# A masked attention and rational feed-forward kernel: the rational function in pieces of 2048 columns, small VectorE chains put into the order link by link, and new order tables

## The chip, the core and the metric

The program runs on one core of one Trainium2 chip. The metric is the device time of one execution in microseconds; the median of three runs of the kernel before is 1252.32 us (1250.29 to 1256.62). Lower is better. Five engines matter: PE (TensorE, matrix products; its weight loads are listed apart as PEld), DVE (VectorE), ACT (ScalarE), POOL (GpSimd) and SP (SyncE, which here only issues transfers).

## What is computed

Attention over 8 batches of 8 heads, 576 positions, 64 values a head, in which scores below the row's maximum less tau are dropped, and after it a feed-forward layer whose activation is a rational function:

```python
scores = scale * np.matmul(q, k.transpose(0, 1, 3, 2))
thresh = np.max(scores, axis=-1, keepdims=True) - tau
scores = np.where(scores >= thresh, scores, -1000000000.0)
attn = softmax(scores)                       # written out in the reference
x = (attn @ v).transpose(0, 2, 1, 3).reshape(4608, 512)
h = x @ w_in                                 # 512 -> 2048
P = a[0] + a[1] * h + a[2] * h * h + a[3] * h ** 3
Q = 1.0 + abs(b[0]) * abs(h) + abs(b[1]) * h * h
out = (P / (Q + 1e-06)) @ w_out              # 2048 -> 512
```

## The kernel before, in words

**Attention.** A unit is one pair of heads and one block of 128 queries (the last block of a pair holds the 64 remaining queries of both heads). Per unit PE makes the scores (L938, L945, L949), DVE takes the maximum (L955, L957), a small operation makes the threshold (L962 on ACT or L964 on DVE), ACT masks (L970) and exponentiates with a sum (L974), DVE inverts the sum (L985), the weights are split into a high half `hi` (L398 on ACT or L400 on DVE) and a low half (L996 on DVE), two transposing transfers on SP turn them, and PE multiplies by the two halves of V (L1069). For the first units PE itself transposes (L1019, L1024) and multiplies in f32 (L1050).

**Feed-forward.** Work goes by chunks of 256 tokens, and for each chunk by steps of eight blocks of 128 columns of w_in (`NB = 8`). There are 38 steps (the last one of a chunk at the end of the run is cut into smaller ones by `TAIL`). In a step PE makes h in split half precision (L1316), ACT scales it out of the banks (L1326), and then the rational function runs on the step's 2048 columns in *pieces*. Eleven operations make a piece: A (L1333 on ACT or L1335 on DVE), r2 (L1341), q (L1345), r3 (L1355), ln (L1348, ACT), inv (L1351, ACT), e (L1359), n (L1363), g (L1367), gh (L398 on ACT or L400 on DVE) and gl (L1381). All those without an engine named are on DVE. Then PE multiplies by w_out (L1390). `PIECE = 2` makes a piece of 1024 columns, so that a full step has two. The three buffers of a step (h, q, r) come from a pool `t` of seven.

**Scales.** Each chunk has a gain chain: squares (L1175 or L1177), a sum on PE (L1182), a maximum and two bit operations on DVE (L1185, L512, L513), seven one-element operations on POOL (L1198 to L1204), two on DVE (L1209, L1210) and two on POOL (L1244, L1245). The weights' and V's scales end in a chain of six one-element operations on DVE, the function `power` (L501 to L507).

**The order.** Nothing in the program is in the order of the code. Each operation is handed to a planner (`Plan`) with its engine or engines, an assumed duration, a key, what it comes after and which buffers it takes and drops. The planner walks through an imagined time, takes on each engine the startable operation with the smallest key, chooses between ACT and DVE where both are allowed (`FLEX`), and so writes one fixed list for each engine. Wherever its imagined PE stands idle for long enough it puts filler products of the identity matrix into PE's list (`f_warm`, L1557):

```python
n = int((t - free[e]) * WARM / 0.22)     # WARM = 0.6
```

An operation of the planner may hold several instructions; those stand together in the list. Before the change `power` and its relatives are such blocks, for instance

```python
nc.vector.tensor_reduce(cn[:, i:i + 1], bank(hb), AX.X, ALU.max)
power(cn[:, i:i + 1], place(hs)[:, 2:3], 14, sw[:, i:i + 1], ...)
sd = op("DVE", 1.735, key + K["cs"], f_cs, [sd], [hs], [hb, hs])
```

Of the kernel before, what the change touches and what calls it, by code (L numbers as in the profile page):

```python
# [88 lines left out]
K = {"f1": 3.009, "f2": 0.12, "f4": -0.954, "f6": -9.013, "load": -13.706, "junk": 0.862, "sq": 0.34, "cn": -8.632, "cs": 0.764,  # L89
     "s1": -0.486, "s2": -1.589, "wh": 6.869, "wl": -2.379, "wc": -5.563, "vl": 2.383, "vc": 7.9, "vh": 4.017, "qk": -0.767,  # L90
     "max": -2.213, "thr": -0.29, "pre": -0.907, "sum": 2.6, "rec": 2.33, "rec2": -0.863, "diag": -3.135, "tr": -4.968,
# [4 lines left out]

SHIFT_STEPS = {0: -0.394, 1: 4.873, 2: -2.335, 3: -0.077, 4: 1.467, 5: -1.25, 6: -0.993, 7: 1.754, 8: -0.124, 9: 1.878,
# [3 lines left out]

SHIFT_UNITS = {0: -1.536, 1: 0.546, 2: 0.586, 3: 0.677, 4: 1.109, 5: 0.804, 6: -5.595, 7: -0.393, 8: -6.844, 9: -1.995,
# [20 lines left out]
LAM = 0.375  # L123

START = {"ACT": 4.989, "DVE": 3.836}
START_END = 94.259
EARLY = {"ACT": 1.437, "DVE": 3.934}
EARLY_END = 3405.643
PRICE = {"ACT": 1.353, "DVE": 13.322}

TOL = {"PE": 0.066, "ACT": 0.0, "DVE": 0.045, "POOL": 0.1, "DMA": 0, "GD": 0}
# [2 lines left out]
SHARE, SET_OUT, LANDS = (1.47, 0.75), 1.22, (0.68, 1.5)
# [213 lines left out]
def masked_attention_rational_ffn(  # L348
# [119 lines left out]
    def monic():  # L468

        t, u, a3 = (co_[:, i:i + 1] for i in range(6, 9))
        nc.vector.tensor_scalar(t, b0, 2.0 ** -40, TINY, ALU.mult, ALU.max)
        nc.vector.tensor_tensor(t, b1, t, ALU.max)
        nc.vector.reciprocal(u, t)
        nc.vector.tensor_tensor(bc, b0, u, ALU.mult)
        nc.vector.tensor_scalar(qc, u, QC, None, ALU.mult)
        nc.vector.tensor_reduce(t, cf[:, 0:3], AX.X, ALU.max, apply_absolute_value=True)
        nc.vector.tensor_scalar(t, t, TINY, TINY, ALU.mult, ALU.max)  # L480
        nc.vector.tensor_scalar(osc, cf[:, 3:4], 0.0, 2.0, ALU.is_ge, ALU.mult)
        nc.vector.tensor_scalar(osc, osc, -1.0, None, ALU.add)
        nc.vector.scalar_tensor_tensor(a3, cf[:, 3:4], osc, t, ALU.mult, ALU.max)
        nc.vector.tensor_tensor(a3, a3, osc, ALU.mult)
        nc.vector.scalar_tensor_tensor(osc, a3, -1.0, u, ALU.mult, ALU.mult)
        nc.vector.reciprocal(a3, a3)
        nc.vector.tensor_scalar(co_[:, 0:3], cf[:, 0:3], a3, None, ALU.mult)

        nc.vector.tensor_scalar(co_[:, 12:14], co_[:, 3:5], TINY, None, ALU.max)
        nc.vector.reciprocal(co_[:, 12:14], co_[:, 12:14])  # L490
        nc.vector.tensor_single_scalar(co_[:, 9:12].bitcast(I32), co_[:, 0:3].bitcast(I32), 0x7FFFFFFF, ALU.bitwise_and)
# [4 lines left out]
    def power(square, p2, up, inv, s):

# [8 lines left out]
        if s is not None:  # L506
            nc.vector.reciprocal(s, inv)  # L507
# [1092 lines left out]
```

## Time and profile before

| | before |
|---|---|
| median of 3 runs, us | 1252.32 |
| the profiled execution's own time, us | 1245.89 |
| its span, first to last instruction, us | 1243.8 |
| granted TensorE clock, mean | 0.999 |
| PE busy, us (share of the span) | 1201.5 (97%) |
| DVE busy | 1188.5 (96%) |
| ACT busy | 1139.5 (92%) |
| POOL busy | 383.2 (31%) |

The profiled execution is 6.4 us below the median of the runs and 2.1 us lie outside its span. A profile row names the line, the engine, the operation, the tiles as out<-in, their shape, the count, the busy time and the mean duration of one instruction; behind it the idle time of the engine just ahead of these and what ended it. The profile's durations of neighbouring instructions on DVE and ACT overlap a little, so that what one instruction costs its engine is read from start to start in the timeline.

### The profile page before, as it was taken

The page shows a single profiled execution, that of the slowest core. Times are in us where ns is not written, and L with a number is a line of the kernel's source. Part 1 is how long each engine was busy: PE and PEld are TensorE (multiplying, and loading weights), DVE is VectorE, ACT ScalarE, POOL GpSimd, SP SyncE. Part 2 cuts the span into 40 slices and gives each one's busy share as a digit, 9 for nine tenths or more (in the row PEclk, how much of TensorE's full clock was granted, in tenths as well). Part 3 has the DMA queues.
Part 4 walks back from the last instruction along what each step waited for, and adds up shares of the span by engine and source line. Part 5 has one row for each costly group of instructions (what it writes and reads, how often), then busy time and mean ns, then how long its engine had stood idle before and what let it go on. Part 6 is the DMA issues. An engine that isn't in the chain of part 4 may idle for free. (4 is left out here: it accounts for less than half of the span.)

```text
span 1243.8 us, 25741 instructions
## 1 busy us (share of the span) xinstructions
PE 1201.5 (97%) x9537; PEld 791.3 (64%) x9542; DVE 1188.5 (96%) x1733; ACT 1139.5 (92%) x2174; POOL 383.2 (31%) x651
## 2 busy tenths in 40 slices
PE   8887899999999999999999999999999999999998
PEld 6556566566666656756666666665756575766754
DVE  6999989999999999999999999999999999999976
ACT  7999999999999999999988999999999799989733
POOL 2220313153042521524044333343416261710300
PEclk9999999999999999999999999999999999999999
DMA  7662264668467675566525575667655665524300
GB/s 231 208 224 91 84 140 81 129 144 168 83 119 139 132 153 93 121 133 131 103 65 102 119 166 112 131 127 143 144 93 123 109 139 125 108 54 84 66 18 17
DMA packets 341484, 147.75 MB, mean 119 GB/s; under 512 B 314224, under 2 KB 325424, under 8 KB 341360
## 3 DMA queue, kind: packets, MB, share of 16 engines
q1 hardware_dynamic: 320944, 92.06, 39.5%
q0 software_dynamic: 20096, 53.47, 15.1%
q8 instruction: 75, 1.23, 0.4%
q10 hardware_dynamic: 320, 0.59, 0.2%
q14 instruction: 49, 0.40, 0.1%
HBM read 54.69 MB, written 9.44 MB: 52 GB/s over the span
## 5 line engine op out<-in xcount | busy, mean ns | idle before, releaser
L1390 PE MATMUL banks<-wp,t 128*128 128x512 f16 x1728 | 394.9, 380 | 3.8 <-DVE t L1381 3.6
L1316 PEld LDWEIGHTS <-wi 128*128 128x128 f16 x3456 | 333.5, 98 | 76.0 <-issue 23.9
L1316 PE MATMUL banks<-x,wi 128*128 128x256 f16 x3072 | 360.8, 273 | 3.8 <-ACT t L1326 3.1
L1390 PEld LDWEIGHTS <-t 128*128 128x128 f16 x1728 | 163.6, 98 | 204.3 <-issue 22.2
L970 ACT ACTIVATE e<-banks,st 128x576 f32<-128x576 f32 x288 | 210.9, 740 | 14.4 <-DVE st L964 7.5
L974 ACT ACTIVATE e<-e,cf 128x576 f32<-128x576 f32 x288 | 222.7, 781 | 0.1
L996 DVE SCALAR_TENSOR_TENSOR e<-e,st,hi 128x576 f16<-128x576 f32 x252 | 201.7, 809 | 2.5 <-ACT hi L398 2.4
L955 DVE TENSOR_REDUCE st<-banks 128x2 f32<-128x1152 f32 x128 | 172.4, 1348 | 9.0 <-PE banks L949 8.1
L398 ACT ACTIVATE hi<-e,st 128x576 f16<-128x576 f32 x221 | 169.6, 773 | 7.9 <-DVE st L985 4.9
L949 PE MATMUL banks<-KK,QQ 64*128 64x512 f32 x512 | 144.6, 641 | 0.0
L1069 PEld LDWEIGHTS <-V 128*64 128x64 f16 x2520 | 103.7, 111 | 56.4 <-issue 52.9
L1069 PE MATMUL banks<-pT,V 128*64 128x256 f16 (+1 forms) x2520 | 120.8, 249 | 3.9 <-DMA pT<-e 1.2
L1326 ACT ACTIVATE t<-banks,hsc 128x512 f32<-128x512 f32 (+1 forms) x192 | 107.1, 582 | 13.3 <-PE banks L1316 11.4
L1348 ACT ACTIVATE t<-t,co 128x1024 f32<-128x1024 f32 (+1 forms) x73 | 82.9, 1137 | 20.6 <-DVE t L1345 16.3
L1341 DVE SCALAR_TENSOR_TENSOR t<-t,co 128x1024 f32<-128x1024 f32 (+1 forms) x73 | 92.0, 1260 | 4.8 <-ACT t L1326 4.8
L1359 DVE SCALAR_TENSOR_TENSOR t<-t,co,t 128x1024 f32<-128x1024 f32 (+1 forms) x73 | 92.1, 1262 | 3.5 <-ACT t L1351 3.4
L1355 DVE SCALAR_TENSOR_TENSOR t<-t,co,t 128x1024 f32<-128x1024 f32 (+1 forms) x73 | 92.1, 1261 | 0.1
L1367 DVE SCALAR_TENSOR_TENSOR t<-t,co,t 128x1024 f32<-128x1024 f32 (+1 forms) x73 | 91.9, 1260 | 0.1
L1345 DVE SCALAR_TENSOR_TENSOR t<-t,co 128x1024 f32<-128x1024 f32 (+1 forms) x73 | 91.9, 1260 | 0.0
L1381 DVE SCALAR_TENSOR_TENSOR t<-t,gsc,t 128x1024 f16<-128x1024 f32 (+1 forms) x73 | 90.8, 1260 | 0.2
L1363 DVE SCALAR_TENSOR_TENSOR t<-t,t 128x1024 f32<-128x1024 f32 (+1 forms) x73 | 87.6, 1201 | 0.3
L1333 ACT ACTIVATE t<-t 128x1024 f32<-128x1024 f32 x72 | 75.7, 1052 | 1.8 <-DVE t L1381 1.5
(184 smaller groups left out, 1614.8 us busy)
## 6 DMA issues: line engine op xcount, KB each, us to landing
KK<-in_kT_dram POOLq DMA_DIRECT2D x94, 144.0 KB, 2.9
t<-in_w_in_dram POOLq DMA_DIRECT2D x8, 1024.0 KB, 6.1
t<-in_w_out_dram POOLq DMA_DIRECT2D x8, 1024.0 KB, 5.7
V<-in_v_dram POOLq DMA_DIRECT2D x24, 256.0 KB, 3.4
out_dram<-u POOLq DMA_DIRECT2D x24, 256.0 KB, 3.1
V<-u SPq DMA_DIRECT2D x28, 160.0 KB, 2.9
QQ<-in_qT_dram POOLq DMA_DIRECT2D x61, 64.0 KB, 2.6
KK<-in_kT_dram SPq DMA_DIRECT2D x24, 144.0 KB, 2.9
```

Source lines behind the costliest of these rows:

```text
L398: nc.scalar.activation(dst, src, AF.Identity, scale=factor)
L949: nc.tensor.matmul(d, QQ[r, t * P:(t + 1) * P], KK[r, REM:S], **one)
L955: nc.vector.tensor_reduce(box["st"][:, 0:2], box["both"], AX.X, ALU.max, negate=True)
L970: nc.scalar.activation(ev(hh), box["s"][hh], AF.Prelu, scale=SCALE, bias=box["st"][:, 2 + hh:3 + hh], alpha=STEEP)
L974: nc.scalar.activation(e, e, AF.Exp, scale=passes, accum_out=box["st"][:, 4 + hh:5 + hh])
L996: nc.vector.scalar_tensor_tensor(box["lo"][:, c], ev(hh), box["st"][:, 6 + hh:7 + hh], box["hi"][:, c], ALU.mult, ALU.subtract)
L1069: nc.tensor.matmul(dst, V[:, c * P + head * D:c * P + (head + 1) * D], rhs, start=c == 0 and n == 0, stop=c == NT and n == 2)
L1316: nc.tensor.matmul(d, wi_tile(c, f0 + j, hl), x[:, c, :], start=c == 0 and n == 0, stop=c == NC - 1 and n == 2)
L1326: nc.scalar.activation(box["h3"][:, 2 * k:2 * k + 2, sl], psv[:, :, sl], AF.Identity, scale=hsc[:, b2, g:g + 1])
L1355: nc.vector.scalar_tensor_tensor(r, r, a1, cols("h", x), ALU.add, ALU.mult)
L1359: nc.vector.scalar_tensor_tensor(q, q, qc, cols("h", x), ALU.add, ALU.mult)
L1390: nc.tensor.matmul(acc[tt], g[x][:, o:o + P], wo_tile(f, y), start=begins and j == n == 0, stop=ends and j == nb - 1 and n == 2)
```

## The change

Three things are edited.

1. A step's piece is the whole step, 2048 columns, while the step's due position `p` lies between 20 and 12 before the end (positions are counted in units); before and after that it stays 1024. In the list this holds for 26 of the 38 steps.
2. The small DVE chains (`power`, `root`, `monic`, the floor of a gain, the scales of the halves) are handed to the planner link by link through a new function `chain`, each link with 0.07 us, so that other instructions can stand between the links.
3. All tables that set the order are new: K, the shifts of units and steps, the choice prices, the tolerances, the spacing and the due times. POOL's gain operation is now counted as 8.0 us, not 6.6.

```diff
-LEAD, SPACE0, SPACING = 4.456, 6.048, 3.976
-ENDK, ENDS = 2.12, 37.814
+LEAD, SPACE0, SPACING = 6.118, 6.048, 3.976
+ENDK, ENDS = -0.032, 34.052
...
+WHOLE = (20.0, 12.0)
...
-K = {"f1": 3.009, "f2": 0.12, "f4": -0.954, "f6": -9.013, "load": -13.706, "junk": 0.862, "sq": 0.34, "cn": -8.632, "cs": 0.764,
+K = {"f1": 2.797, "f2": 0.725, "f4": -0.963, "f6": -8.948, "load": -20.533, "junk": -0.978, "sq": 0.616, "cn": -8.354,
...
-LAM = 0.375
+LAM = 22.894
...
-PRICE = {"ACT": 1.353, "DVE": 13.322}
+PRICE = {"ACT": 0.0, "DVE": 7.397}
...
+    def chain(key, parts, after=(), take=(), first=(), last=()):
+        o = None
+        for n, (dur, fn) in enumerate(parts):
+            o = op("DVE", dur, key, fn, after if o is None else [o], take if n == 0 else (),
+                   (*(first if n == 0 else ()), *(last if n == len(parts) - 1 else ())))
+        return o
...
-        sd = op("DVE", 1.735, key + K["cs"], f_cs, [sd], [hs], [hb, hs])
+        sd = chain(key + K["cs"], [(0.6, f_cs)] + power(lambda i=i: cn[:, i:i + 1], lambda hs=hs: place(hs)[:, 2:3], 14, sw[:, i:i + 1],
+                                                        sw[:, NW + i:NW + i + 1]), [sd], [hs], [hb], [hs])
...
-        o = op("POOL", 6.6, key, f, [norm_done[ck], ready_all])
+        o = op("POOL", 8.0, key, f, [norm_done[ck], ready_all])
...
-        span = min(PIECE, nb // 2)
+        span = nb // 2 if WHOLE[0] <= p < end - WHOLE[1] else min(PIECE, nb // 2)
```

All lines behind the constants stand 2 to 10 lines lower in the changed file (L1341 is L1346, L1381 is L1386, L996 is L1006, the fillers' L1557 is L1562).

How the lists look now is shown at three places. The first is DVE in the middle of the run, with two steps in work; t are the buffers of the rational function, e and hi those of the attention weights. Before:

```order
L1341 SCALAR_TENSOR_TENSOR t_70<-t_68,co 128x1024
L996 SCALAR_TENSOR_TENSOR e_82<-e_82,st_90,hi_84 128x576
L1359 SCALAR_TENSOR_TENSOR t_69<-t_69,co,t_68 128x1024
L1355 SCALAR_TENSOR_TENSOR t_70<-t_70,co,t_68 128x1024
L1363 SCALAR_TENSOR_TENSOR t_69<-t_69,t_68 128x1024
L955 TENSOR_REDUCE st_92<-banks 128x2
L1085 SCALAR_TENSOR_TENSOR xr_100<-banks,xr_100 128x64
L985 RECIPROCAL st_91<-st_91 128x2
L1367 SCALAR_TENSOR_TENSOR t_70<-t_70,co,t_69 128x1024
```

And the changed kernel at about the same place of DVE's list:

```order
L1368 SCALAR_TENSOR_TENSOR t_69<-t_69,t_73 128x2048
L1346 SCALAR_TENSOR_TENSOR t_74<-t_71,co 128x2048
L965 TENSOR_REDUCE st_89<-banks 128x2
L1095 SCALAR_TENSOR_TENSOR x_99<-banks,x_99 128x256
L995 RECIPROCAL st_88<-st_88 128x2
L1372 SCALAR_TENSOR_TENSOR t_72<-t_72,co,t_69 128x2048
L1006 SCALAR_TENSOR_TENSOR e_82<-e_82,st_88,hi_84 128x576
L402 TENSOR_SCALAR t_69<-t_72,gsc 128x2048
```

Two instructions of 1024 columns have become one of 2048, with the attention's instructions still between them.

The second place is DVE near the start, where the scale of the first quarter of w_in is made (cn is its maximum, sc a scratch column, sw the scale). Before:

```order
L669 TENSOR_REDUCE cn<-banks 128x1
L501 TENSOR_SCALAR sc_96<-cn 128x1
L502 TENSOR_SCALAR sc_96<-sc_96 128x1
L503 TENSOR_SCALAR sc_96<-sc_96 128x1
L504 TENSOR_SCALAR sc_96<-sc_96 128x1
L505 TENSOR_SCALAR sw<-sc_96 128x1
L507 RECIPROCAL sw<-sw 128x1
```

Now the same chain begins like this:

```order
L679 TENSOR_REDUCE cn<-banks 128x1
L974 TENSOR_SCALAR st_92<-st_92,cf 128x2
L484 TENSOR_TENSOR co<-cf,co 128x1
L511 TENSOR_SCALAR sc_96<-cn 128x1
L965 TENSOR_REDUCE st_93<-banks 128x2
L394 COPY pT_86<-banks 128x128
L974 TENSOR_SCALAR st_93<-st_93,cf 128x2
L485 RECIPROCAL co<-co 128x1
L608 TENSOR_SCALAR t_70<-t_70 128x1024
L609 SCALAR_TENSOR_TENSOR t_70<-t_70 128x1024
L486 TENSOR_TENSOR co<-cf,co 128x1
L512 TENSOR_SCALAR sc_96<-sc_96 128x1
```

Its last link, the reciprocal that makes sw, stands 43 rows behind its first; before it stood 6 rows behind.

The third place is the end of PE's list, ahead of the last 96 products with w_out (wp), where the last products with w_in are followed by fillers. Before:

```order
L1316 LDWEIGHTS wi
L1316 MATMUL banks<-x_97,wi 128x256
L1557 MATMUL banks<-ident 128x128 x12
L1390 LDWEIGHTS t_74
L1390 MATMUL banks<-wp_140,t_74 128x512
```

Now:

```order
L1321 LDWEIGHTS wi
L1321 MATMUL banks<-x_97,wi 128x256
L1562 MATMUL banks<-ident 128x128 x20
L1395 LDWEIGHTS t_70
L1395 MATMUL banks<-wp_140,t_70 128x512
```

The fillers there have become 20 instead of 12. Over the whole list they have become 187 instead of 113 (each is two instructions in the profile); the other products are the same in number.

Counted over DVE's and ACT's lists, the choice between the two engines has moved too: DVE has 55 of the hi halves instead of 31 (ACT 197 instead of 221), 10 of V's high halves instead of 1, and a few more squares and copies.

More of the change, by code (lines that the diff above doesn't have):

```diff
@@ L87 @@
         "wh": {"ACT": 1.05, "DVE": 0.662}, "o": {"ACT": 0.569, "DVE": 0.663}, "twice": {"ACT": 0.135, "DVE": 0.085}}
[L89 to L91 removed]
[4 rows of a table removed]
[L97 removed]
[3 rows of a table removed]
[L102 removed]
[17 rows of a table removed]
[L121 to L131 removed]
+K = {"f1": 2.797, "f2": 0.725, "f4": -0.963, "f6": -8.948, "load": -20.533, "junk": -0.978, "sq": 0.616, "cn": -8.354,
+     "cs": 0.987, "s1": -1.221, "s2": -1.43, "wh": 6.761, "wl": -3.231, "wc": -5.093, "vl": 3.197, "vc": 8.526, "vh": 4.112,
+     "qk": -1.83, "max": -2.533, "thr": -0.274, "pre": -0.08, "sum": 2.714, "rec": 2.615, "rec2": -1.882, "diag": -2.221,
[4 rows of a table added]
+SHIFT_STEPS = {0: -0.763, 1: 3.182, 2: -1.673, 3: -0.999, 4: 4.589, 5: -1.503, 6: -0.54, 7: 0.729, 8: 0.129, 9: 1.147, 10: 1.923,
[3 rows of a table added]
+SHIFT_UNITS = {0: 1.354, 1: 2.223, 2: -1.996, 3: 1.114, 4: 2.442, 5: -5.821, 6: -6.72, 7: -0.245, 8: -8.681, 9: -1.949,
[17 rows of a table added]
+SHIFT_OPS = {}
+LAM = 22.894
+START = {"ACT": 5.277, "DVE": 3.841}
+START_END = 94.296
+EARLY = {"ACT": 2.779, "DVE": 4.995}
+EARLY_END = 3836.486
+PRICE = {"ACT": 0.0, "DVE": 7.397}
+TOL = {"PE": 0.077, "ACT": 0.013, "DVE": 0.0, "POOL": 0.1, "DMA": 0, "GD": 0}
 WARM, WARM_END = 0.6, 1e9
[L134 removed]
+SHARE, SET_OUT, LANDS = (1.47, 0.75), 1.22, (0.9, 1.5)
 LANES, LANE = 8, 0.03
@@ L475, in monic @@
[L475 to L491, printed above, removed]
@@ L492, in monic @@
-        nc.vector.tensor_tensor(g0, g0, rqc, ALU.mult)
-    co = op("DVE", 2.8, 6.0, monic, [co])
-    def power(square, p2, up, inv, s):
-        bits = p2.bitcast(I32)
-        nc.vector.tensor_scalar(bits, square.bitcast(I32), 0x7F800000, 1, ALU.bitwise_and, ALU.logical_shift_right)
-        nc.vector.tensor_scalar(bits, bits, 0x1FC00000, None, ALU.add)
-        nc.vector.tensor_single_scalar(bits, bits, 0x7F800000, ALU.bitwise_and)
-        nc.vector.tensor_scalar(p2, p2, 2.0 ** -40, 2.0 ** 100, ALU.max, ALU.min)
-        nc.vector.tensor_scalar_mul(inv, p2, 2.0 ** -up)
-        if s is not None:
-            nc.vector.reciprocal(s, inv)
+        v = nc.vector
@@ new lines, in monic @@
+        return [(0.07, f) for f in (
+            lambda: v.tensor_scalar(t, b0, 2.0 ** -40, TINY, ALU.mult, ALU.max),
+            lambda: v.tensor_tensor(t, b1, t, ALU.max),
+            lambda: v.reciprocal(u, t),
+            lambda: v.tensor_tensor(bc, b0, u, ALU.mult),
+            lambda: v.tensor_scalar(qc, u, QC, None, ALU.mult),
+            lambda: v.tensor_reduce(t, cf[:, 0:3], AX.X, ALU.max, apply_absolute_value=True),
+            lambda: v.tensor_scalar(t, t, TINY, TINY, ALU.mult, ALU.max),
+            lambda: v.tensor_scalar(osc, cf[:, 3:4], 0.0, 2.0, ALU.is_ge, ALU.mult),
+            lambda: v.tensor_scalar(osc, osc, -1.0, None, ALU.add),
+            lambda: v.scalar_tensor_tensor(a3, cf[:, 3:4], osc, t, ALU.mult, ALU.max),
+            lambda: v.tensor_tensor(a3, a3, osc, ALU.mult),
+            lambda: v.scalar_tensor_tensor(osc, a3, -1.0, u, ALU.mult, ALU.mult),
+            lambda: v.reciprocal(a3, a3),
+            lambda: v.tensor_scalar(co_[:, 0:3], cf[:, 0:3], a3, None, ALU.mult),
+            lambda: v.tensor_scalar(co_[:, 12:14], co_[:, 3:5], TINY, None, ALU.max),
+            lambda: v.reciprocal(co_[:, 12:14], co_[:, 12:14]),
+            lambda: v.tensor_single_scalar(co_[:, 9:12].bitcast(I32), co_[:, 0:3].bitcast(I32), 0x7FFFFFFF, ALU.bitwise_and),
+            lambda: v.tensor_tensor(g0, g0, rqc, ALU.mult),
+        )]
@@ new lines, in masked_attention_rational_ffn @@
+    co = chain(6.0, monic(), [co])
+    def power(square, p2, up, inv, s):
+        v = nc.vector
+        return [(0.07, f) for f in (
+            lambda: v.tensor_scalar(p2().bitcast(I32), square().bitcast(I32), 0x7F800000, 1, ALU.bitwise_and, ALU.logical_shift_right),
+            lambda: v.tensor_scalar(p2().bitcast(I32), p2().bitcast(I32), 0x1FC00000, None, ALU.add),
+            lambda: v.tensor_single_scalar(p2().bitcast(I32), p2().bitcast(I32), 0x7F800000, ALU.bitwise_and),
+            lambda: v.tensor_scalar(p2(), p2(), 2.0 ** -40, 2.0 ** 100, ALU.max, ALU.min),
+            lambda: v.tensor_scalar_mul(inv, p2(), 2.0 ** -up),
+            lambda: v.reciprocal(s, inv))]
@@ L509, in root @@
     def root(dst, square):
[L512 to L513 removed]
+        v = nc.vector
+        return [(0.07, f) for f in (
+            lambda: v.tensor_single_scalar(dst.bitcast(I32), square.bitcast(I32), 1, ALU.logical_shift_right),
+            lambda: v.tensor_scalar(dst.bitcast(I32), dst.bitcast(I32), 0x1FC00000, None, ALU.add))]
@@ L537, in f3 @@
             nc.vector.tensor_reduce(box["m2"], box["all"], AX.X, ALU.max)
-            power(box["m2"], box["p2"], up, inv, s)
         o = op("DVE", 0.08, key, f1, after, [h])
@@ L542, in scale_ops @@
         o = op("PE", 0.22, key, f_all, [o], [hb], [hd])
-        return op("DVE", 1.34, key, f3, [o], (), [h, hb])
+        return chain(key, [(0.2, f3)] + power(lambda: box["m2"], lambda: box["p2"], up, inv, s), [o], (), [hb], [h])
     NW = DFF // WS
@@ L1190, in norm_ops @@
         o = plan.pe("hh", 0.44, key + K["norm"], f_norm, [o], [hb], [hq])
-        norm_done[ck] = op("DVE", 0.712, key + K["root"], f_root, [o], (), [hb])
+        norm_done[ck] = chain(key + K["root"], [(0.335, f_root)] + root(w[:, 1:2], w[:, 0:1]), [o], (), [hb])
     def bound(w, x, sigma):
@@ L1206, in floor_ops @@
     def floor_ops(w, key, after):
-        def f():
-            p, q = w[:, 4:5], w[:, 5:6]
-            nc.vector.tensor_single_scalar(p.bitcast(I32), p.bitcast(I32), 0x7F800000, ALU.bitwise_and)
-            nc.vector.reciprocal(q, p)
-        return op("DVE", 0.26, key, f, [after])
+        p, q = w[:, 4:5], w[:, 5:6]
+        return chain(key, [(0.07, lambda: nc.vector.tensor_single_scalar(p.bitcast(I32), p.bitcast(I32), 0x7F800000, ALU.bitwise_and)),
+                           (0.07, lambda: nc.vector.reciprocal(q, p))], [after])
     def first_gain(ck, i, key):
@@ L1225, in first_gain @@
         plan.rank = key
-        o = op("POOL", 6.6, key, f, [norm_done[ck], half_done[i]])
+        o = op("POOL", 8.0, key, f, [norm_done[ck], half_done[i]])
         return op("POOL", 2.6, key, f_out, [floor_ops(w, key, o)])
```

39 lines of the change are left out of this document (16 added, 23 removed), and 48 rows, old and new, of tables (K, SHIFT_STEPS, SHIFT_UNITS).

## Prediction

> **What bounds the kernel now.** I read the page's busy times first, then busy time by stage, then the waits inside the long middle stage, and last the timeline at single places, for what an instruction costs its engine.
>
> The page's first part and the view by windows (start, first units with the weights, middle, end; behind the stretch its length, then PE, PEld, DVE, ACT and POOL busy with instruction counts, clock, DMA share):
>
> ```profile
> PE 1201.5 (97%) x9537; PEld 791.3 (64%) x9542; DVE 1188.5 (96%) x1733; ACT 1139.5 (92%) x2174; POOL 383.2 (31%) x651
> ```
>
> ```profile
> 0.00:31.00 31.00, 27.57 (x174) 20.09 (x176) 21.07 (x54) 22.38 (x45) 6.77 (x27) 1.00 0.78 230
> 31.00:155.00 124.00, 103.59 (x781) 73.70 (x786) 117.72 (x250) 121.89 (x229) 24.91 (x45) 0.99 0.46 153
> 155.00:1181.00 1026.00, 1012.83 (x8254) 664.89 (x8255) 1006.95 (x1384) 972.91 (x1876) 346.88 (x571) 1.00 0.59 118
> 1181.00:1243.80 62.80, 57.52 (x334) 32.59 (x332) 42.73 (x48) 22.27 (x27) 4.64 (x9) 1.00 0.05 17
> ```
>
> Until 155 us ACT binds (121.89 of 124.00) with DVE close behind, and PE idles 20 us. In the middle, four fifths of the run, two engines are full at once: PE 1012.83 and DVE 1006.95 of 1026.00. ACT has 53 us to spare there. So an instruction taken off DVE alone can bring at most what PE leaves open, 13.2 us of idle time and the fillers. The fillers in the middle, by the same view for the tile ident on PE:
>
> ```profile
> 155.00:1181.00 1026.00, 12.05 (x80) 1.00 0.59 118
> ```
>
> In the middle PE thus loses about 13.2 + 12.05 = 25 us, DVE 19 us. Who waits for whom in the middle, the waits that this change can touch (engine, line, what it waited for, us in total, times, longest):
>
> ```profile
> PE banks L945 <- ACT e L970: 5.0, 7, 1.4
> PE banks L1390 <- DVE t L1381: 2.3, 2, 1.3
> ...
> DVE e L996 <- ACT hi L398: 2.4, 5, 1.0
> DVE gt L1209 <- POOL gt L1204: 2.0, 3, 1.0
> ...
> ACT t L1348 <- DVE t L1345: 8.9, 8, 4.3
> ```
>
> No wait is large; each engine runs a list of its own and the lists fit each other closely.
>
> **What merging the pieces removes.** The timeline of DVE shows the cost from start to start, shorter than the printed duration (start, duration, instruction):
>
> ```profile
> 317.34 0.52 DVE L400 TENSOR_SCALAR hi<-e,st 128x576 f16<-128x576 f32 x1
> 317.77 1.28 DVE L1345 SCALAR_TENSOR_TENSOR t<-t,co 128x1024 f32<-128x1024 f32 x1
> 318.97 0.81 DVE L996 SCALAR_TENSOR_TENSOR e<-e,st,hi 128x576 f16<-128x576 f32 x1
> ...
> 1186.85 1.21 DVE L1363 SCALAR_TENSOR_TENSOR t<-t,t 128x1024 f32<-128x1024 f32 x1
> 1187.98 1.27 DVE L1359 SCALAR_TENSOR_TENSOR t<-t,co,t 128x1024 f32<-128x1024 f32 x1
> ...
> 1224.51 0.69 DVE L1363 SCALAR_TENSOR_TENSOR t<-t,t 128x512 f32<-128x512 f32 x1
> 1225.12 1.27 DVE L1381 SCALAR_TENSOR_TENSOR t<-t,gsc,t 128x1024 f16<-128x1024 f32 x1
> ...
> 1228.64 0.74 DVE L1355 SCALAR_TENSOR_TENSOR t<-t,co,t 128x512 f32<-128x512 f32 x1
> 1229.31 0.74 DVE L1345 SCALAR_TENSOR_TENSOR t<-t,co 128x512 f32<-128x512 f32 x1
> ```
>
> 1024 columns cost 1.20 us (317.77 to 318.97) and 512 cost 0.67 (1228.64 to 1229.31): 0.53 for each 512 more, so 2048 should cost 1.20 + 1.06 = 2.26, an estimate, against 2.40 for two of 1024. Six of the seven operations save 0.14; L1363 (1.13 and 0.61) saves 0.09. A step saves 0.93, and 26 steps 24 us. The bounds are 0 (a long instruction costs two short ones) and these 24; I take 24, since two sizes of the same lines lie on it.
>
> [...]
>
> On ACT the same way, from the groups by form and from a stretch of ACT's timeline:
>
> ```profile
> L1351 ACT ACTIVATE t<-t 128x1024 f32<-128x1024 f32 x71 | 75.0, 1056 | 0.2
> ...
> L1351 ACT ACTIVATE t<-t 128x512 f32<-128x512 f32 x2 | 1.3, 630 | 0.1
> ```
>
> ```profile
> 301.72 1.16 ACT L1348 ACTIVATE t<-t,co 128x1024 f32<-128x1024 f32 x1
> 302.76 0.79 ACT L398 ACTIVATE hi<-e,st 128x576 f16<-128x576 f32 x1
> 303.43 0.31 ACT L962 ACTIVATE st<-st,cf 128x2 f32<-128x2 f32 x1
> ```
>
> 512 columns more take 0.426 us, and neighbours overlap by 0.12 (L1348 lasts 1.16, the next starts after 1.04; a hi half costs 0.67). So one of 2048 for two of 1024 saves 2 x 0.94 - (0.94 + 0.85) = 0.09 in A and inv, and 2 x 1.04 - (1.04 + 0.85) = 0.19 in ln, and in gh if it is like ln: 0.56 a step, 14 us in 26 steps.
>
> **What the new choice of engines moves.** By the counts of the lists, 24 hi halves go from ACT to DVE, and nine of V's high halves, whose group row on ACT is
>
> ```profile
> L398 ACT ACTIVATE u<-V,sx 128x640 f16<-128x640 f32 x27 | 22.2, 829 | 0.3 <-DVE sx L507 0.3
> ```
>
> On DVE a hi half costs 0.43 (317.34 to 317.77 above): 24 x 0.43 = 10.3 us. V's have 640 columns for 576: 9 x 0.48 = 4.3, an estimate. Some thirty more instructions (squares, gh of five whole steps, reciprocals' additions, copies) of 0.1 to 1.2 us I put at 13 us, an estimate from their kinds, with bounds of 3 and 30. DVE takes over 28 us where the merging freed 24: **DVE +4 us**, and it is still full. ACT loses 24 x 0.67 = 16, 9 x (0.829 - 0.12) = 6, about 18 for the rest, and the 14 above: about 54 us, from the engine that had room. That is the main point: the change frees ACT, not DVE, and PE's products are the same in number.
>
> What ACT's relief is worth is bounded by the waits for ACT: PE 5.0 and DVE 2.4 in the middle, not additive, and 5.5 us in the ACT-bound stage (54 us spread evenly, 124 of 1244). Most of those waits come from the position in the lists, not from load. I take **-4 us**, between 0 and -13.
>
> **The fillers.** One is two instructions and costs PE
>
> ```profile
> 431.69 2.17 PE L1557 MATMUL banks<-ident 128*128 128x128 f32 x18
> 435.21 0.49 PE L945 MATMUL banks<-KK,QQ 128*128 128x128 f32 x2 [1.35 <-ACT e L970]
> ```
>
> 2.17 / 9 = 0.24 us. Here they stood where PE had to wait anyway: 1.35 us of waiting came on top. 74 more fillers are 18 us of PE time at most. By their places about a third are in the first 155 us, where PE idles 20 us and they are hidden; if that cover is gone they cost 6 us. About thirty lie in the middle, 7 us; where the rational result is late anyhow they cost nothing, where it is not they hold back the full PE. I take **+2 us** for the middle, bounds 0 and +7. At the end:
>
> ```profile
> 1205.01 9.99 PE L1316 MATMUL banks<-x,wi 128*128 128x256 f16 x90
> 1214.83 2.84 PE L1557 MATMUL banks<-ident 128*128 128x128 f32 x24
> 1217.87 0.39 PE L1390 MATMUL banks<-wp,t 128*128 128x512 f16 x1 [0.19 <-ACT t L398]
> 1219.34 20.68 PE L1390 MATMUL banks<-wp,t 128*128 128x512 f16 x95 [1.08 <-DVE t L1381]
> ```
>
> Here nothing else is left for PE: the last chunk's gain chain, which starts from sums that PE makes just ahead of the first row, and the gl behind it set 1219.34. In the new list 18 fewer products with w_in stand behind those sums, and 8 more fillers; 18 x 9.99 / 90 = 2.0 us less cover. **+2 us**, bounds 0 and +4.
>
> **The chains link by link.** They save no instruction. The first w_in scale is ready 43 rows after its maximum instead of 6; between stand bulk instructions of 0.4 to 1.3 us, and whoever needs the scale (s1, s2, then the first products with w_in) waits for that. But the rows in between are work that DVE had to do anyway and ACT binds that stage. I take 0, bounds -4 and +8.
>
> **The sum** is +4 - 4 + 2 + 2 + 0 = +4. Against the profiled execution's own 1245.9 (span 1243.8 and 2.1 around it) that makes 1249.9. That execution lies 6.4 below the median of the runs, 1252.3, so for the median I forecast 1252.3 + 4 = **1256 us**. What a measurement of this kernel can tell from no change is 0.5%, 6.3 us: 1246.0 to 1258.6.
>
> **Rivals.**
>
> *ACT's relief is worth all of its bound* (faster). If the waits for ACT go in both stages (-5.0 - 2.4 - 5.5 = -12.9) and DVE's sum is 0 rather than +4, with the fillers of the middle inside real waits and the end 1 us later, the time is 1252.3 - 12.9 + 1 = 1240. For it: ACT is the fullest engine until 155 us, and 20 us of PE idleness lie there. Against it: DVE is nearly as full there and takes ACT's work.
>
> *PE waits for whole pieces* (slower). With two pieces the first products with w_out can begin after the first piece's gl; with one piece they wait for eleven operations on 2048 columns. The planner's own picture shows this: 74 more fillers. If they are all lost, 74 x 0.24 = 18 us, the time is 1270. It decides as soon as the next step's 96 products with w_in (90 took 9.99 us) are done before gl ends. For it: PE and DVE are both full, so no slack exists to catch up. Against it: the wait for gl is only 2.3 us in the middle now, and two steps are always in work.
>
> *POOL's gain chain is held up by longer DVE instructions* (slower). One-element operations on POOL take very different times (duration min, median, max in ns):
>
> ```profile
> L1201 POOL TENSOR_SCALAR gt<-gt,co x20: 334/341/4134, 146.7 to 1207.4; 128x1 f32<-128x1 f32 x20
> ```
>
> So something blocks them now and then for longer than a DVE instruction of 1.2 us. With blockers of 2.26, each of seven might wait half of 1.06 more, 3.7 us a gain; where DVE already waits for POOL (three times, 2.0 us) that is exposed: 3 x 3.7 = 11 us, 1263. [...] Against it: the chain is started ahead of need.
>
> **How the numbers follow.** The forecast 0.36, its own range 1246 to 1258.5 from the terms' bounds taken half; the first rival 0.30; the second 0.26; the third 0.08. So faster by more than 0.5% has 0.30, within 0.5% 0.36, slower 0.34. The range takes in most of the two rivals at 1240 and 1270 with some of their unknowns: 1236 to 1274, about one in ten outside at either end.
>
> **What would show it.** Right: L1346 to L1386 at 2048 columns start 2.2 to 2.3 us before the next instruction; DVE's busy time within 10 us of 1188 and ACT's down by some 50 to 80 by the printed durations; the middle still with PE and DVE above 97%. Wrong towards faster: PE's idle time in the first 155 us clearly below 20 us, or the waits for ACT gone and PE's with them. Wrong towards slower: waits of L1395 for gl (L1386) well above 2.3 us in the middle, fillers followed by no wait, or POOL's gain operations longer with DVE's L1217 waiting for them. If 2048 columns cost 2.4 us, the first term is wrong, and the time would be near 1276.

## The result and the profile after

The changed kernel takes 1266.27 us (median of four runs, 1264.70 to 1268.06), the kernel before beside it 1252.34: a ratio of 1.0123 [1.0105, 1.0141], 13.9 us slower by the medians and 15.4 by the ratio. The profiled execution of the changed kernel took 1265.44 us with a span of 1263.2, against 1245.89 and 1243.8: 19.4 us more span to account for; that this is more than 13.9 is mostly because the profiled execution of the kernel before lies 6.4 us below the median of its runs. One execution of a kernel below, the changed kernel with free products with w_out, ran at a granted clock of 0.555 and took 2015.8 us; neither its time nor its rows are used. The forecast was 1256, the rival with late products 1270.

The busy times of the whole span (first part of the page, changed kernel):

```profile
PE 1224.9 (97%) x9685; PEld 813.9 (64%) x9690; DVE 1185.4 (94%) x1608; ACT 1098.8 (87%) x2013; POOL 396.4 (31%) x651
```

DVE's load has fallen by 3.1 us and ACT's by 40.7. PE is busy 23.4 us longer with the same products. The same four stretches as in the prediction (length, busy PE, PEld, DVE, ACT, POOL, granted clock, DMA share, GB/s):

```profile
0.00:31.00 31.00, 27.83 (x172) 20.66 (x174) 20.51 (x45) 21.78 (x45) 7.62 (x27) 1.00 0.77 230
31.00:155.00 124.00, 111.33 (x841) 81.51 (x842) 119.06 (x274) 115.89 (x218) 31.62 (x45) 0.93 0.45 153
155.00:1181.00 1026.00, 1009.73 (x8170) 663.33 (x8165) 990.35 (x1230) 925.55 (x1711) 352.90 (x568) 1.00 0.60 117
1181.00:1263.20 82.20, 76.00 (x515) 48.40 (x512) 55.44 (x62) 35.60 (x43) 4.30 (x12) 0.98 0.04 14
```

The last stretch is 82.20 us long for 62.80 before: all of the 19.4 us shows there. But that is where work lands that wasn't done earlier, and one has to take the fillers out to see it. The fillers alone (the tile ident on PE), changed kernel:

```profile
0.00:155.00 155.00, 23.07 (x162) 0.94 0.52 168
155.00:1181.00 1026.00, 23.98 (x166) 1.00 0.60 117
1181.00:1263.20 82.20, 5.57 (x46) 0.98 0.04 14
```

and before (the middle stands in the prediction, 12.05):

```profile
0.00:155.00 155.00, 19.48 (x122) 0.99 0.53 168
...
1181.00:1243.80 62.80, 2.84 (x24) 1.00 0.05 17
```

In the middle PE did 1009.73 - 23.98 = 985.75 us of real products, before 1012.83 - 12.05 = 1000.78: **15.0 us less in the same 1026 us**, 11.9 of them for more fillers and 3.1 for more idle time (16.27 for 13.17). The end had those 15.0 to catch up: real products 76.00 - 5.57 = 70.43 for 54.68, 15.75 more by busy time (0.75 beyond the backlog; a stretch of half clock, shown below, is in it), fillers 2.73 more and idle time 0.9 more. 15.0 + 4.4 = 19.4. Up to 155 us nothing was lost: 172 + 841 - 162 = 851 products stand there for 833 before (over the whole span both profiles have 9311), in spite of a lower granted clock, 0.93 for 0.99 between 31 and 155 us.

So PE lost its time in the middle, where fillers fill what the planner expects to be idle time. Who is late there? PE's own waits in the middle, changed kernel (what waited for what, us in total, times, longest):

```profile
PE banks L1079 <- DMA pT<-e: 5.0, 5, 1.7
PE banks L955 <- ACT e L980: 3.3, 7, 0.8
PE banks L1321 <- ACT t L1331: 2.4, 4, 1.4
PE banks L1395 <- DVE t L1386: 2.4, 2, 1.7
PE banks L1079 <- DVE st L965: 2.3, 1, 2.3
```

The wait of the products with w_out (L1395) for gl is as long as before, 2.4 for 2.3. What has grown is the wait of the products with V (L1079, before L1069) for the transposed weights; before it was, with 1.1 us more for the transfers of hi,

```profile
PE banks L1069 <- DMA pT<-e: 1.2, 2, 1.0
```

ACT's waits in the middle tell where that comes from; before:

```profile
ACT st L962 <- DVE st L955: 9.4, 13, 2.5
...
ACT hi L398 <- DVE st L985: 4.9, 4, 2.9
...
ACT x L1079 <- PE banks L1069: 4.4, 7, 0.9
```

and in the changed kernel:

```profile
ACT st L972 <- DVE st L965: 23.6, 30, 2.0
ACT hi L400 <- DVE st L995: 17.3, 20, 2.0
ACT x L1089 <- PE banks L1079: 14.8, 12, 3.7
```

ACT waits 30 times for a row maximum (L965) where it waited 13 times, and 20 times for a reciprocal (L995) where it waited 4 times. Those two rows are 40.9 us for 14.3, 26.6 us more; with the third, in which ACT waits for PE, they are 55.7 for 18.7, 37 us more, most of the 40.7 us that the change took off ACT. A stretch of DVE shows how such a wait comes about (start, duration, instruction):

```profile
717.22 2.34 DVE L1346 SCALAR_TENSOR_TENSOR t<-t,co 128x2048 f32<-128x2048 f32 x1
719.48 1.35 DVE L965 TENSOR_REDUCE st<-banks 128x2 f32<-128x1152 f32 x1
...
720.88 2.33 DVE L1360 SCALAR_TENSOR_TENSOR t<-t,co,t 128x2048 f32<-128x2048 f32 x1
...
723.33 0.81 DVE L1006 SCALAR_TENSOR_TENSOR e<-e,st,hi 128x576 f16<-128x576 f32 x1
724.06 2.28 DVE L1368 SCALAR_TENSOR_TENSOR t<-t,t 128x2048 f32<-128x2048 f32 x1
726.26 0.15 DVE L995 RECIPROCAL st<-st 128x2 f32<-128x2 f32 x1
```

with two instructions of ACT that use the maximum and the reciprocal (in brackets the idle time ahead of them and what ended it):

```profile
720.87 0.30 ACT L972 ACTIVATE st<-st,cf 128x2 f32<-128x2 f32 x1 [1.60 <-DVE st L965]
...
726.45 0.78 ACT L400 ACTIVATE hi<-e,st 128x576 f16<-128x576 f32 x1 [1.47 <-DVE st L995]
```

and, soon after, a transposing transfer (SPq is SP's queue) and a wait of PE:

```profile
724.90 1.20 SPq L1016 DMA_TRANSPOSE pT<-e  x1
...
729.10 0.35 PE L1079 MATMUL banks<-pT,V 128*64 128x64 f16 x10 [1.69 <-DMA pT<-e]
```

A reciprocal of 0.15 us stands behind an instruction of 2048 columns, and ACT waits 1.47 for it before it can make the high half. PE's wait that ends at 729.10 doesn't come from that reciprocal: the high half of 726.45 was made after the transfer of 724.90 had been issued. It fits a like place a little earlier, where a low half (L1006 at 723.33) stands behind another instruction of 2048 columns (L1360) and its transfer behind it. That this is the way in which the time is lost is so far only read; the experiments test it.

### The profile page after: what moved, and what is told of

The parts are those of the page before. It is cut to its first block, busy times and chain, and to the rows that moved or that the text cites. A ratio compares the mean times of both kernels' runs of the same rounds, so it can differ in the third digit from the quotient of the medians.

```text
span 1263.2 us, 25751 instructions
## 1 busy us (share of the span) xinstructions
PE 1224.9 (97%) x9685; PEld 813.9 (64%) x9690; DVE 1185.4 (94%) x1608; ACT 1098.8 (87%) x2013; POOL 396.4 (31%) x651
## 5 line engine op out<-in xcount | busy, mean ns | idle before, releaser
L1395 PE MATMUL banks<-wp,t 128*128 128x512 f16 x1728 | 396.7, 380 | 4.9 <-DVE t L1386 3.4
L1395 PEld LDWEIGHTS <-t 128*128 128x128 f16 x1728 | 165.5, 99 | 203.9 <-issue 22.3
L980 ACT ACTIVATE e<-banks,st 128x576 f32<-128x576 f32 x288 | 208.3, 737 | 13.5 <-DVE st L974 8.0
L1006 DVE SCALAR_TENSOR_TENSOR e<-e,st,hi 128x576 f16<-128x576 f32 x252 | 202.1, 809 | 4.3 <-ACT hi L400 3.4
L965 DVE TENSOR_REDUCE st<-banks 128x2 f32<-128x1152 f32 x128 | 172.6, 1348 | 12.7 <-PE banks L959 11.3
L400 ACT ACTIVATE hi<-e,st 128x576 f16<-128x576 f32 x197 | 149.6, 769 | 18.9 <-DVE st L995 17.3
L1079 PEld LDWEIGHTS <-V 128*64 128x64 f16 x2520 | 104.2, 111 | 57.6 <-issue 51.8
L1079 PE MATMUL banks<-pT,V 128*64 128x256 f16 (+1 forms) x2520 | 121.9, 250 | 7.4 <-DMA pT<-e 5.0
L1346 DVE SCALAR_TENSOR_TENSOR t<-t,co 128x2048 f32<-128x2048 f32 (+2 forms) x47 | 86.6, 1843 | 8.4 <-ACT t L1331 8.3
L1364 DVE SCALAR_TENSOR_TENSOR t<-t,co,t 128x2048 f32<-128x2048 f32 (+2 forms) x47 | 86.6, 1846 | 4.4 <-ACT t L1356 4.4
L782 POOL DMA_DIRECT2D QQ<-in_qT_dram x47 | 26.4, 561 | 202.8 <-PE banks L948 132.3
L1353 ACT ACTIVATE t<-t,co 128x2048 f32<-128x2048 f32 (+2 forms) x47 | 75.1, 1599 | 16.8 <-DVE t L1350 12.2
L1372 DVE SCALAR_TENSOR_TENSOR t<-t,co,t 128x2048 f32<-128x2048 f32 (+2 forms) x47 | 86.5, 1843 | 0.2
L1360 DVE SCALAR_TENSOR_TENSOR t<-t,co,t 128x2048 f32<-128x2048 f32 (+2 forms) x47 | 86.6, 1842 | 0.0
L1386 DVE SCALAR_TENSOR_TENSOR t<-t,gsc,t 128x2048 f16<-128x2048 f32 (+2 forms) x47 | 86.1, 1843 | 0.4 <-ACT t L400 0.2
L1350 DVE SCALAR_TENSOR_TENSOR t<-t,co 128x2048 f32<-128x2048 f32 (+2 forms) x47 | 86.3, 1841 | 0.1
L1368 DVE SCALAR_TENSOR_TENSOR t<-t,t 128x2048 f32<-128x2048 f32 (+2 forms) x47 | 83.6, 1782 | 0.1
```

The lines of the kernel that those rows point to most:

```text
L400: nc.scalar.activation(dst, src, AF.Identity, scale=factor)
L965: nc.vector.tensor_reduce(box["st"][:, 0:2], box["both"], AX.X, ALU.max, negate=True)
L980: nc.scalar.activation(ev(hh), box["s"][hh], AF.Prelu, scale=SCALE, bias=box["st"][:, 2 + hh:3 + hh], alpha=STEEP)
L1006: nc.vector.scalar_tensor_tensor(box["lo"][:, c], ev(hh), box["st"][:, 6 + hh:7 + hh], box["hi"][:, c], ALU.mult, ALU.subtract)
L1079: nc.tensor.matmul(dst, V[:, c * P + head * D:c * P + (head + 1) * D], rhs, start=c == 0 and n == 0, stop=c == NT and n == 2)
L1346: nc.vector.scalar_tensor_tensor(cols("r", x), h, a2, h, ALU.add, ALU.mult)
```

## The experiments

All kernels were timed in three rounds beside the kernel before. Their time is given as median and as ratio to the kernel before, with its 95% interval; 0.001 is 1.25 us.

### Without most of the fillers

The first theory is that the fillers themselves hold PE back: 74 more of them, and several that end with no wait behind them. Both kernels lose all fillers after 40 us of the planner's time:

```diff
-WARM, WARM_END = 0.6, 1e9
+WARM, WARM_END = 0.6, 40.0
```

Of 187 fillers 38 are left in the changed kernel, of 113 in the kernel before 34.

> The changed kernel with the same lists, but fillers only where the planner's time is below 40 us: 38 of them for 187, all those of the middle and the end are gone. PE's idle time is the same in both profiles (73 and 75 us), and the fillers grew by 16.6 us, nearly all of the 19.4 us that the span grew. If the fillers themselves hold PE back, as many of them are followed at once by the next product, the time falls by 10 us or more, to 1256 or less. If they only fill real waits for the rational function, the waits grow in their place and the time stays at 1263 to 1269.

> The kernel before with fillers only below 40 us of the planner's time: 34 for 113. It spends 17 us of PE time on the fillers that go. If fillers hold PE back wherever they stand, it gains nearly in proportion, 8 to 15 us, to 1238 to 1244, and the difference to the changed kernel with few fillers stays about 10. If its fillers lie in real waits (most are followed by a further wait in the profile), it stays at 1249 to 1256, and only the changed kernel gains.

Measured: changed kernel 1277.20 us, 1.0197 [1.0164, 1.0229]; kernel before 1260.61 us, 1.0069 [1.0046, 1.0092]. Both are slower without them, by 11 and 8 us, above every range that was expected, so that fillers as a net loss are ruled out. Real waits take the place of most of them, and the granted clock falls, in the profiled executions from 0.991 to 0.976 and from 0.999 to 0.984. Over the whole span of the changed kernel PE's fillers fall by 40.8 us (52.6 to 11.8), its idle time grows by 31.6 (38.3 to 69.9), and the same products take 19.5 us longer (1172.3 to 1191.7). In the kernel before these are 23.4, 19.6 and 20.3. So about 9 us of the changed kernel's fillers covered no wait, about 4 of the other's, and what makes the kernels slower without fillers is that their products run longer at the lower clock. The waits can be read now that no filler covers them. In the middle of the changed kernel without fillers:

```profile
PE banks L955 <- ACT e L980: 10.6, 10, 2.6
PE banks L1321 <- ACT t L1331: 6.8, 5, 3.8
PE banks L1079 <- DMA pT<-e: 5.8, 4, 2.9
PE banks L1395 <- DVE t L1386: 5.8, 5, 2.0
PE banks L1079 <- DMA KK<-in_kT_dram: 2.8, 1, 2.8
PE banks L1395 <- ACT t L400: 2.4, 1, 2.4
```

and of the kernel before without fillers:

```profile
PE banks L945 <- ACT e L970: 13.0, 10, 3.4
PE banks L1316 <- ACT t L1326: 2.2, 6, 0.9
PE banks L1069 <- DMA pT<-e: 1.7, 3, 1.0
PE banks L1069 <- DMA pT<-hi: 1.1, 2, 0.7
...
PE banks L1390 <- DVE t L1381: 1.1, 1, 1.1
...
PE banks L1390 <- ACT t L398: 0.7, 1, 0.7
```

Three kinds of products wait longer in the changed kernel: those with w_out for gl and gh (8.2 us for 1.8; the 2.8 in an expectation below counts 1.0 more that a transfer of K ended), those with V (8.6 for 2.8; 2.8 of the 8.6 were ended by a transfer of K), and those with w_in for a free bank (6.8 for 2.2). Which of them costs the time can't be told from the rows, since one delay begets the next.

### The same order with halves

This undoes the merging alone: every operation on 2048 columns stays where it is in the lists and issues two instructions of 1024.

```diff
+        def halves(x):
+            return [(k, min(k + PIECE, x[1])) for k in range(x[0], x[1], PIECE)]
...
-                return lambda: f(x)
+                return lambda: f(x) if f in (f_gh, f_gl) else [f(y) for y in halves(x)]
```

> The changed kernel with the same order of operations, but each operation on 2048 columns issues two instructions of 1024 in its place. It undoes the saving alone: DVE gets 24 us more, ACT 14 us more. If the middle is no longer bound by DVE (it is idle 36 us of 1026 there, for 19 before), the time grows by less than 8 us, to at most 1274. If DVE still binds, it grows by 16 to 25 us, to 1282 to 1291.

Measured: 1279.06 us, 1.0224 [1.0196, 1.0252], so 12.6 us (by the ratios, give or take 4) above the changed kernel, between the two ranges expected. DVE is busy 1204.60 us in it for 1185.35 in the changed kernel, ACT 1113.10 for 1098.82: the merging takes 19.3 us off DVE, not 24, and 14.3 off ACT, as estimated. In this order the merging is a gain of about 13 us, two thirds of the DVE time that it saves; so the rest of the change, that is the links, the choice of engines and the new order together, costs about 27. ACT waits for the maxima here too:

```profile
ACT st L972 <- DVE st L965: 31.1, 37, 2.4
```

With two instructions of 1024 at the same place ACT waits 31.1 us, with one of 2048 23.6. Here the wait follows the place in the list, not the merging.

### Pieces of 1024 in the changed code

```diff
-WHOLE = (20.0, 12.0)
+WHOLE = (1e9, 12.0)
-WARM, WARM_END = 0.6, 1e9
+WARM, WARM_END = 0.6, 40.0
```

> The changed kernel with pieces of 1024 columns throughout, the new tables, chains link by link, fillers only below 40 us; the planner writes a new order for it. If whole pieces cost PE waits by their length, this one is faster than the changed kernel with few fillers, by 5 to 15 us. If the tables fit whole pieces alone, it is slower than it by 10 us or more.

Measured: 1323.79 us, 1.0574 [1.0552, 1.0596], 47 us above the changed kernel with few fillers. With twice as many operations of half the length and the same tables the planner writes an order in which nothing fits. The run tells only that: the tables belong to one set of operations, and a part of this change can't be had with the tables of the whole.

### Each part with tables of its own

So the parts were tried with tables searched anew for each, by small random steps on the planner's own total, each a short search. Three started from the tables of the kernel before: the control, which is that kernel with the new assumed durations alone (8.0 us for POOL's gain operation, `LANDS` 0.9 for 0.68); the chains link by link, with pieces of 1024 and the old durations; and whole pieces without the links, with the old durations. The fourth has links, pieces of 1024 and the new durations, and started from the changed kernel's tables. The edit of the third:

```diff
-        span = min(PIECE, nb // 2)
+        span = nb // 2 if WHOLE[0] <= p < end - WHOLE[1] else min(PIECE, nb // 2)
```

> The control: the kernel before with pieces of 1024 and chains in blocks, only the two assumed durations of the changed kernel (POOL's gain operation 8.0, landing 0.9) and order tables that a short random search set anew for them. Its list of PE has 117 fillers for 113. If an order that was set anew costs nothing by itself, it takes 1250 to 1256 us; if any new order of this length of search is worse on the chip, 1259 or more.

> The kernel before with the chains handed over link by link, pieces of 1024, and order tables set anew by the same search; 120 fillers in PE's list. If links with other work between them hold up the scales and with them PE, it is slower than the control by 5 us or more; if chains cost nothing, as predicted, it lies within 5 us of the control, at 1249 to 1260.

> The kernel before with whole pieces of 2048 in the middle, chains in blocks, and order tables set anew by the same search; 154 fillers. DVE has 15 us less work than before by the lists. If whole pieces make PE wait for gl and for what stands behind the long instructions, it is slower than the control by 8 to 16 us, about 1260 to 1268, with DVE idle more; if DVE's saving is worth its size, it is faster than the control.

> The changed kernel with pieces of 1024 and order tables from the changed kernel's, set anew by a search of the same kind; 207 fillers, more than the changed kernel's 187. If the number of fillers in the list tells how long PE waits, it is as slow as the changed kernel or slower, 1265 to 1275, and the tables and not the pieces set the time. If whole pieces are what costs, it is faster than 1260.

| kernel | us | ratio to before |
|---|---|---|
| control | 1254.81 | 1.0030 [1.0011, 1.0049] |
| chains link by link | 1261.22 | 1.0094 [1.0076, 1.0112] |
| whole pieces | 1275.64 | 1.0192 [1.0173, 1.0212] |
| links, pieces of 1024, from the changed tables | 1272.84 | 1.0177 [1.0159, 1.0195] |

The control lies within what was expected if a new order costs nothing. The chains alone cost 8 us against the control by the ratios (0.0064, give or take 0.0027; 6.4 by the medians), whole pieces alone 20 (0.0162), more than the 8 to 16 expected. The middle of the control, and of the kernel with whole pieces:

```profile
155.00:1181.00 1026.00, 1007.92 (x8155) 660.65 (x8153) 995.70 (x1374) 968.99 (x1864) 339.93 (x566) 1.00 0.60 117
```

```profile
155.00:1181.00 1026.00, 1000.00 (x8074) 654.62 (x8072) 977.07 (x1215) 931.82 (x1701) 346.42 (x568) 0.99 0.59 116
```

DVE has 18.6 us less to do there. PE does 7.9 us less, and without the fillers (16.20 and 25.05 us) 16.8 us less of real products, as the changed kernel did 15.0 less. ACT's wait for the row maxima in the control:

```profile
ACT st L936 <- DVE st L929: 9.6, 16, 1.3
```

and with whole pieces:

```profile
ACT st L938 <- DVE st L931: 19.6, 27, 2.0
```

It doubles, with quite other tables than the changed kernel's, and the longest has grown from 1.3 to 2.0 us. But the wait isn't the price by itself: the kernel before has 9.4, the changed one 23.6, and whole pieces with 19.6 are slower than the changed kernel. The fourth kernel of the table has pieces of 1024 and waits much less than the changed one:

```profile
ACT st L946 <- DVE st L939: 15.1, 22, 2.3
```

Yet at 1272.84 it is 7 us slower than the changed kernel by the ratios (0.0054, give or take 0.0026), as was expected for the case that the tables and not the pieces set the time. In its middle PE does 979.8 us of real products (1006.60 less 26.78 of fillers). Nor is PE's wait for transposed weights the price by its row: the control has more of it than the changed kernel, and loses little.

```profile
PE banks L1043 <- DMA pT<-e: 6.4, 5, 2.8
```

None of these four is faster than the kernel before. The search was short, and how much of each time is the tables' fault stays open.

### Products that wait for nothing

The last four take waits away by other data, in the kernels with few fillers, where the waits can be seen. In the first pair the products with w_out in the middle take their stationary side from a resident piece of w_out instead of gh and gl; in the second pair the products with V besides take a resident piece of V instead of the transposed weights, so that the transposing transfers no longer wait for those products to give their buffers back either. All other work is done, in the same order; the output isn't the reference's.

```diff
-                nc.tensor.matmul(acc[tt], g[x][:, o:o + P], wo_tile(f, y), start=begins and j == n == 0,
+                t = wo_tile(f, 0)[:, 0:P] if 20.0 <= p < end - 12.0 else g[x][:, o:o + P]
+                nc.tensor.matmul(acc[tt], t, wo_tile(f, y), start=begins and j == n == 0,
...
-                            rhs = pT[:, :, lo, c if hh == 0 or c == NT else NT + 1 + c, :]
+                            rhs = VH[:, 0:2 * P].rearrange("p (u k) -> p u k", u=2)
...
-                            rhs = pT[:, 0, lo, c, hh * REM:(hh + 1) * REM]
+                            rhs = VH[:, 0:REM]
```

> The changed kernel without most fillers (the kernel of the first experiment), and in the middle of the run the products with w_out take their stationary side from a resident part of w_out in place of gh and gl: all work is still done, but no product waits for the rational function, and no buffer of a step waits for those products. The output is not the reference's. Without this edit the kernel takes 1277.2 us, and the products with w_out wait 8.2 us for gh and gl in the middle (2.8 in the kernel before treated alike). Theory 1 (whole pieces make PE late): the waits for gh and gl go and most of the lost time with them, 1261 to 1268 us, 9 to 16 less. Theory 2 (all of the order fits less well; the wait for gl is one of several of equal weight): only the wait itself goes, 1268 to 1272, or it turns into waits for e, h and the transposing transfers and less than 5 us are gained.

> The same edit on the kernel before without most fillers (1260.6 us without the edit). Both theories: the waits for gh and gl were 2.8 us there, so 1256 to 1260 us. What tells them apart is the difference between this run and the changed kernel with the same edit, 16.6 us without it: under 8 by theory 1, 11 or more by theory 2.

> As the changed kernel with free products with w_out, and besides the products with V take a resident part of V in place of the transposed weights, so that they wait neither for the softmax nor for the transposing transfers. The output is not the reference's. The waits for those transfers were 8.6 us in the middle without fillers (2.8 in the kernel before). Theory 1: little is left to gain, 0 to 5 us less than with free products with w_out alone. Theory 2: as much again as by the first edit, 5 to 9 us.

> The same two edits on the kernel before without most fillers. Both theories: 1 to 4 us less than with free products with w_out alone. The difference to the changed kernel with both edits: by theory 1 the same as with one edit, by theory 2 smaller by about 6 us, and what then remains (the first stage and the end) 2 to 8 us.

| waits taken away | changed kernel, us | kernel before, us | difference |
|---|---|---|---|
| none | 1277.20 | 1260.61 | 16.6 |
| for gh and gl | 1277.90, 1.0213 [1.0177, 1.0249] | 1260.03, 1.0078 [1.0050, 1.0107] | 17.9 |
| and for the transposed weights | 1265.91, 1.0113 [1.0083, 1.0144] | 1257.88, 1.0052 [1.0029, 1.0074] | 8.0 |

Free products with w_out bring nothing in either kernel (in the changed one 0.0016 more, give or take 0.005), where theory 1 expected 9 to 16 us in the changed one. The theory that PE is late because whole pieces make gl late has fallen: without those 8.2 us of waiting the time is the same. Where they went can't be read, since this variant has no rows. Free products with V bring 12.0 us in the changed kernel (0.0100, give or take 0.0047), more than the 5 to 9 of theory 2, and 2.1 in the kernel before, less than its margin, and the difference between the two falls from 17.9 to 8.0 (by the intervals, 10 give or take 7). PE's waits in the middle that are left in the changed kernel:

```profile
PE banks L955 <- ACT e L980: 17.4, 13, 4.3
```

The waits of L1079 and L1395 are gone, and part of them has moved to the scores, whose banks ACT (L980) must free first. ACT's waits for DVE's maxima and reciprocals are still there, but no product with V depends on them any more. So without fillers about half of the difference, with a wide margin, is tied to the products with V: to weights that reach them late, or to buffers that they give back late. The edit doesn't tell these two apart: in the kernel with few fillers the transposing transfers (L1016) wait for the products with V as well, and with free products that row is gone too.

```profile
SPq L1016 <- PE banks L1079: 82.9, 34, 11.2
```

The other 8 us weren't resolved. That the same share holds with the fillers in place is argued, not shown, and so is that whole pieces, and not the new order, make these products late: the kernel with whole pieces alone has a new order too. Products with V freed alone weren't tried.

## Why the prediction was right in range and too low

The measured 1266.27 lies in the stated range of 1236 to 1274, but not in the forecast's own range of 1246 to 1258.5. It was caught because the range was stretched to a rival whose mechanism was wrong, and that is luck. The forecast took the change for a matter of load on DVE and ACT, with 2 us for PE's fillers in the middle; the time was lost there. Of the signs that were named ahead, the start-to-start time (2.26) and DVE's busy time (1185.4) came out as forecast. ACT fell by 40.7 and not by 50 to 80, and DVE's share in the middle is 96.5% and not above 97%.

**DVE +4.** The size of the operation was right: 717.22 to 719.48 is 2.26 us, the estimate to the hundredth. The rows' saving of 0.14 us an instruction stands at single places; over the kernel with halves it is 19.3 us for 182 instructions, 0.11 each. With 19.3 saved, DVE took over about 16 us from ACT and not 28, so its load fell by 3.1 instead of rising by 4. If load had set the time, the kernel would have been faster than forecast. It was 10 us slower. (Without any saving the sum would have been 1256 + 24 = 1280; the recorded 1276 is an error of addition.)

**ACT's relief -4.** ACT lost 40.7 us where 54 were forecast, and no gain of PE from it is seen in the middle. The sentence that the waits come from the place in the lists and not from load was right, and the value of -4 ran against it: 26.6 us of the relief became waiting for DVE and 10.4 waiting for PE. The first rival (1240) fell with it.

**Fillers and waits in the middle +2.** This is the step that failed. It put about thirty of the 74 more fillers into the middle, where 43 of them stand, and took them to be harmless or a loss in themselves, bounded by 7 us. They cost 11.9 us of PE time there and idle time 3.1. They were no loss on balance: without most of them the kernel is 11 us slower, and 31.6 of their 40.8 us come back as idle time. They are the planner's own picture of how much PE would have to wait, and that picture was right in direction. The prediction had it in hand (74 more fillers) and read it only as the second rival's.

**The second rival, 1270** (chance 0.26), had the size, +18 for a measured +13.9, and the victim, PE; its mechanism was wrong. The products with w_out wait for gl as long as before (2.4 for 2.3 us), and freed from it the time is the same without fillers. What stands behind the long instructions and is waited for is attention: the row maximum, the reciprocal, and through them the halves, the transposing transfers and the products with V. How much of the 13.9 us goes this way, and how much is the new order itself, stays open: the halves show only that the rest of the change costs more than the merging gains.

In the changed kernel DVE is no longer full (990.35 of 1026.00) and others wait for it; but breaking up its instructions in place cost 12.6 us. In the kernel before the small operations stand between the parts, at 1252.34 us; but so they do in the fourth of the kernels with tables of their own, at 1272.84.

**The third rival (POOL), 1263**, didn't occur. The operation shown in the prediction, L1201, is L1210 now (duration min, median, max in ns):

```profile
L1210 POOL TENSOR_SCALAR gt<-gt,co x20: 335/341/3785, 142.1 to 1224.2; 128x1 f32<-128x1 f32 x20
```

It lasts far longer than its median of 0.34 us at times, as before (longest 3.8 us for 4.1). The one behind it lasted 5.3 us at most (before 2.1). That DVE's instructions hold these operations up, and by 3.7 us a gain, is shown by no run; the seven together take 5.5 us in the mean for 5.8 before, and DVE, which waited 2.0 us in the middle for this chain, has no wait for it any more. The planner now counts 8.0 us for the chain.

**The end +2** was +4.4: 2.73 for fillers, 0.9 of idle time, and 0.75 of products beyond the backlog, in which a stretch of half clock lies. The last 96 products start like this:

```profile
1229.64 4.63 PE L1562 MATMUL banks<-ident 128*128 128x128 f32 x40
1235.73 0.39 PE L1395 MATMUL banks<-wp,t 128*128 128x512 f16 x1 [1.46 <-ACT t L400]
1237.14 22.36 PE L1395 MATMUL banks<-wp,t 128*128 128x512 f16 x95 [1.03 <-DVE t L1386]
```

The 95 take 22.36 us where they took 20.68. The half clock was not foreseen.

**The chains link by link, 0** (bounds -4 and +8). In the changed kernel no loss shows up to 155 us; alone, with tables of their own, they cost 8 us against the control, the upper bound. The two don't agree, the profile of the kernel with chains shows no loss (it is of an execution of 1255.31 us, the lowest of four), and the share of the tables isn't known.

## What to carry to other kernels

A longer instruction on an engine that several chains share saved time of its own here (0.11 us for each of the 182 of 2048 columns), and ACT waited longer for the row maxima in the same list (23.6 us for 9.4), as it did behind two short ones back to back (31.1); price it by who waits for those small operations, and not by the engine's load alone. Where a planner puts in fillers, their number is its forecast of PE's waiting: take it as a rough one (here 154 fillers went with 1276 us, 187 with 1266 and 207 with 1273), and test a suspected wait by giving the waiting products other data before blaming it. Order tables belong to the operations for which they were found, so a part of such a change can only be judged with tables of its own.

## What was not expected of the hardware

Filler products were worth their place in both kernels: taking out most of them cost 8 and 11 us, because in the profiled executions the same products took some 20 us longer at the lower granted clock (0.984 for 0.999, 0.976 for 0.991; 0.015 of 1270 us is 19), and only 4 and 9 us of fillers and idle time were saved.

PE's clock fell to half (0.51) for 3.4 us behind two waits that were both much shorter, 1.46 and 1.03 us. Windows of the changed kernel (busy PE, PEld, DVE, ACT, POOL, then the granted clock), ahead of and in the last 96 products:

```profile
1225.00:1237.50 12.50, 10.01 (x87) 8.91 (x86) 11.38 (x13) 7.73 (x9) 0.82 (x4) 1.00 0.00 1
1237.50:1240.90 3.40, 3.40 (x10) 1.18 (x8) 3.29 (x4) 1.95 (x4) 0.00 (x0) 0.51 0.00 0
1240.90:1245.00 4.10, 4.10 (x21) 1.86 (x19) 3.86 (x7) 1.45 (x2) 0.00 (x0) 1.00 0.01 2
```

In 1237.50 to 1240.90 PE is busy all the time at a granted clock of 0.51, after waits of 1.46 and 1.03 us. Both together are 2.49 us within 2.9 us, from the end of the fillers at 1234.27 to 1237.14, with one product between them. No run shows what halved the clock, or what brought it back after 3.4 us.
